# The opening of a float32 convolution and mixer kernel, worked in half chunks of two tokens

## The chip, the cores and the metric

The kernel runs on one core of a Trainium2 chip. The metric is the device time of one execution in microseconds (us), lower is better. The time before is the median of three runs.

## What is computed

The inputs are `x` of 8 batches x 4096 tokens x 192 features, `weight_gen` of 8 x 4096 x 8 heads x 7 taps, and four weight matrices that arrive as 64-bit floats. First comes a convolution over the last seven tokens, whose taps are a softmax; then a mixer over tokens and one over channels:

```python
w = softmax(weight_gen)                       # over the 7 taps, per token and head
out[b, s, h, :] = sum_k w[b, s, h, k] * x_pad[b, s + k, h, :]
h = relu(out.T @ w_tok1) @ w_tok2             # over the 4096 tokens, 256 hidden
u = out + h.T
y = u + relu(u @ w_ch1) @ w_ch2               # over the 192 features, 1536 hidden
```

## The kernel before, in words

A chunk is 512 tokens: each of the 128 partitions holds CT = 4 neighbouring tokens of 192 features. There are NCH = 8 chunks in a batch and NG = 64 in all. A main loop over the 64 chunks does the channel mixer on TensorE, and beside it the convolution and token mixing of later batches, in an order that a planner (`pump`) fixes when the program is built. Ahead of the loop stands the **prologue**, which is written out by hand: the convolution of the eight chunks of batch 0, their token mixing `th` (first product), and the conversion of the weights from 64-bit words to 32-bit floats. Each engine (and SyncE's DMA queue, SP, and GpSimd's, POOL) runs its instructions in the order in which this code issues them. Only the prologue and what first follows on it is touched.

For each chunk `m` the prologue of before goes like this.

- `softmax(m)` (L194) makes the taps of two chunks at once: on VectorE a maximum (L201) and a subtraction (L202), on ScalarE the exponential (L203), on VectorE the sum (L204), an addition, a reciprocal and a product (L210). `run(items, softmax(m + 1))` issues it from one place.
- `products(m)` (L344) multiplies the chunk with its taps on VectorE (L350): four taps in one instruction of 3072 elements a partition, three in one of 2304.
- `convert` (L157) turns raw words into floats: three ScalarE instructions (L170, L173, L174) and one on VectorE (L169, the `shift`). `begin` issues the ScalarE part of a weight block two chunks ahead, `run` the rest. Where a float is kept as two parts, `split` follows: a copy on ScalarE, a subtraction on VectorE (L188, L189). `convert_channel` does so for `w1` (three blocks) and `c2` (L495 to L497), `convert_w2` for the second token matrix.
- `sums(m)` (L362) adds the seven taps on TensorE, by 42 transposes that accumulate in PSUM (`tapsum`, L358); ScalarE copies the result to `sum` (L370); `turn_back` (L394) transposes it back, by six transposes, and ScalarE copies that to `xa` (L400).
- `token1_first` (L553) multiplies `xa` with the chunk's token weights on TensorE.
- `keep_sum` (L375) copies the transposed sum a second time from PSUM, by five ScalarE copies that sort the tokens (L388); for chunks 0 and 1 into the tiles `xb_`, from chunk 2 on into `ts`, which ScalarE's own DMA queue stores in DRAM (L391, L392). `load_xt` (L328) brings it back in the main loop.
- SP issues the loads of `x` (`load_x`), of the taps (`load_wg`), of raw weights (`fetch_...`; three raw buffers in turn), and the store `s0` of each converted token block (L959), in the order of the code; it waits where an instruction waits.

After the eight chunks `make_h1` (L507) applies the relu and splits `th` in two parts (L510 on ScalarE, L512 on VectorE), `token2(0)` (L558) makes the second token product (L570), VectorE adds it to chunk 0 (L580 to L582), and the main loop begins. PSUM of the main loop is the prologue's, so L570 waits for the last reader of `tapsum`.

Of the kernel before, what the change touches and what calls it, by code (L numbers as in the profile page):

```python
# [22 lines left out]
def mixer_kernel(ctx: ExitStack, tc: tile.TileContext, x, wg, wt1, wt2, wc1, wc2, out):  # L23
    nc = tc.nc
# [55 lines left out]
    def load_x(m):  # L80
# [12 lines left out]
        nc.gpsimd.memset(t[0:2, 0:PAD, :], 0.0)  # L93
# [22 lines left out]
    staged = {"raw": 0, "val": 0}  # L116
# [28 lines left out]
    def val_tile():  # L145

        n = staged["val"]
        staged["val"] += 1
        pool = pro if pro is not None and n % 6 >= 4 else p1
        return pool.tile([P, NV], F32, tag="val", name="val", bufs=2 if pool is pro else 4)  # L150
# [6 lines left out]
    def convert(raw, n, out):  # L157
# [5 lines left out]
        v = val_tile()[:, 0:n]  # L163
# [176 lines left out]


    KA = 4

    def products(m, pro):  # L344
        src, (wn, j) = xt.pop(m), wnt.pop(m)
        prs = []
        for k0, k1 in ((0, KA), (KA, K)):
            pr = pro.tile([P, KA, CT, D], F32, tag="pr", name="prk", bufs=3)[:, 0:k1 - k0]
            x_k, w = taps(src, wn, j, k0, k1)
            nc.vector.tensor_mul(pr.rearrange("p k t (h g) -> p k (t h) g", h=H), x_k, w)  # L350
            prs += [pr[:, k] for k in range(k1 - k0)]
        return prs

    sumt = {}
# [5 lines left out]
    NB = CT * D // P  # L360

    def sums(m, prs, between=lambda: None):  # L362

        ps = ps_pro.tile([P, 2, 512], F32, tag="sum", name="tapsum", bufs=2).rearrange("p k n -> p (k n)")
        for k, pr in enumerate(prs):
            flat = pr.rearrange("p t d -> p (t d)")
            for j in range(NB):
                transpose(ps[:, j * P:(j + 1) * P], flat[:, j * P:(j + 1) * P], k == 0 and j % 4 == 0)
        sumt[m] = p1.tile([P, CT, D], F32, tag="pr", name="sum", bufs=PR).rearrange("p t d -> p (t d)")
        nc.scalar.copy(sumt[m], ps[:, 0:NB * P])  # L370
        between()
        turn_back(m)
        return ps

    def keep_sum(m, ps):  # L375

        if m < 2:
            t = xbt[m] = xb_[m]
        else:
            t = pro.tile([P, 2, N], F32, tag="ts", name="ts0", bufs=2)  # L380
        to = [t[:, n, :].rearrange("p (n b t c) -> p c t n b" if m == 0 else "p (n t c b) -> p c t n b", c=2, t=2, b=Q)
              for n in range(2)]
        blocks = ps[:, 0:NB * P].rearrange("p (t j n b) -> p j t n b", t=2, n=P // Q, b=Q)
        lo, hi = slice(0, DC), slice(DC, P)
        for c in range(2):
            for n, rows, j, of in ((0, slice(0, P), 0, slice(0, P)), (1, hi, 1, lo)) if c == 0 else \
                    ((0, lo, 1, hi), (0, hi, 2, lo), (1, hi, 2, hi)):
                nc.scalar.copy(to[n][rows, c], blocks[of, j])  # L388
        if m >= 2:
            xst[m] = dram.tile([2, P, N], F32, name=f"xs{m}")  # L390
            nc.scalar.dma_start(xst[m][0], t[:, 0, :])  # L391
            nc.scalar.dma_start(xst[m][1, DC:P], t[DC:P, 1, :])  # L392

    def turn_back(m):  # L394

        t = sumt.pop(m)
        ps = ps_pro.tile([P, 2, 512], F32, tag="turn", name="turn").rearrange("p k n -> p (k n)")
        for j in range(NB):
            transpose(ps[:, j * P:(j + 1) * P], t[:, j * P:(j + 1) * P], j % 4 == 0)
        nc.scalar.copy(new_xa(m).rearrange("p c d -> p (c d)"), ps[:, 0:NB * P])  # L400

# [156 lines left out]
    def token2(m, up=None):  # L558
# [3 lines left out]
        if seeded:  # L562
            up = ps_w.tile([P, 2, 512], F32, tag="w", name="up")
            nc.scalar.copy(up.rearrange("p k (n b c) -> p (k n) c b", c=CT, b=Q),  # L564
                           xb.rearrange("p k (n c b) -> p (k n) c b", c=CT, b=Q))
# [346 lines left out]
    with tc.tile_pool(name="pro", bufs=1) as pro, \  # L912
# [5 lines left out]
        prefetch(0)  # L918
        th = ps_pro.tile([P, 2, 512], F32, tag="th", name="th")

        def token1_first(m, v):
            token1_float(th, v.rearrange("p (c r) -> p c r", c=CT), m,
                         0 if m == 0 else None, CT - 1 if m == NCH - 1 else None)

        def start(items):

            for item in items:
                if item[0] == "v":
                    return chain((item,), items)
                item[2]()  # L930

        begun = {}

        def begin(job, *what):
            v = []
            begun[what] = start(job(*what) if job else convert(rawt.pop(what), CT * R, v)), v

        extra = {2: ("w1", 0), 4: ("w1", 1)}
        run(softmax(0))
        fetch_w1(0)  # L940
        begin(None, "tok", 0)
        prefetch(1)
        fetch_w1(1)
        begin(None, "tok", 1)
        for m in range(NCH):
            prs = products(m, pro)
            if m + AHEAD < NCH:
                prefetch(m + AHEAD)
            items, (v,) = begun.pop(("tok", m))
            run(items, softmax(m + 1) if (m + 1) % SM == 0 and m + 1 < NCH else ())  # L950
            if m + AHEAD < NCH:
                fetch_w1(m + AHEAD)
            if m in extra:
                fetch_channel(*extra[m])
            if m == NCH - 2:
                load_wg(NCH)
                fetch_w2(0)
                fetch_channel("w1", 2)
            nc.sync.dma_start(s0[m], v)  # L959
            if m - 1 in extra:  # L960
                run(begun.pop(extra[m - 1])[0])
            if m < NCH - 1:
                ps = sums(m, prs)
                token1_first(m, v)
                keep_sum(m, ps)
            if m in extra:
                begin(convert_channel, *extra[m])
            if m + AHEAD < NCH:
                begin(None, "tok", m + AHEAD)
            if m == NCH - 2:  # L970
                begin(convert_w2, 0)
                begin(convert_channel, "w1", 2)
        fetch_channel("c2", 0)
        w2_items = begun.pop((0,))[0]
# [213 lines left out]
```

## Time and profile before

| what | us |
|---|---|
| median of three runs | 2113.66 (2111.83 to 2114.88) |
| span of the profiled execution, first to last instruction | 2109.4 |
| the median less that span | 4.3 |
| start of L580, which ends the prologue here | 126.06 |

The page gives no time of its own for the profiled execution beside its span; what lies around the span is taken as the 4.3 us of the table. All starts are counted from the first instruction. Busy is time in an instruction; instructions of one engine overlap by some hundredths of a us.

### The profile page before, as it was taken

The page shows a single profiled execution, that of the slowest core. Times are in us where ns is not written, and L with a number is a line of the kernel's source. Part 1 is how long each engine was busy: PE and PEld are TensorE (multiplying, and loading weights), DVE is VectorE, ACT ScalarE, POOL GpSimd, SP SyncE. Part 2 cuts the span into 40 slices and gives each one's busy share as a digit, 9 for nine tenths or more (in the row PEclk, how much of TensorE's full clock was granted, in tenths as well). Part 3 has the DMA queues.
Part 4 walks back from the last instruction along what each step waited for, and adds up shares of the span by engine and source line. Part 5 has one row for each costly group of instructions (what it writes and reads, how often), then busy time and mean ns, then how long its engine had stood idle before and what let it go on. Part 6 is the DMA issues. An engine that isn't in the chain of part 4 may idle for free.

```text
span 2109.4 us, 32249 instructions
## 1 busy us (share of the span) xinstructions
PE 2049.7 (97%) x12832; PEld 1686.3 (80%) x12832; DVE 1500.4 (71%) x1723; ACT 1449.9 (69%) x2245; POOL 159.5 (8%) x193
## 2 busy tenths in 40 slices
PE   6679999999999999999999999999999999999998
PEld 5667888788887888888888888888888888888887
DVE  6658988888888777777777787777777765343433
ACT  6578766677776676667667667666766766676665
POOL 0001111001101000000000010000100000000000
PEclk9899999999999999999999999999999999999999
DMA  8666767777876776666666666666666564321221
GB/s 321 198 204 189 210 169 227 229 206 204 243 225 165 204 200 172 188 158 181 175 197 174 191 181 167 174 184 200 177 184 191 147 170 140 91 71 49 57 63 23
DMA packets 165078, 363.82 MB, mean 172 GB/s; under 512 B 16456, under 2 KB 104264, under 8 KB 149568
## 3 DMA queue, kind: packets, MB, share of 16 engines
q1 hardware_dynamic: 138240, 284.96, 42.2%
q0 software_dynamic: 25344, 74.46, 18.2%
q10 hardware_dynamic: 1344, 2.36, 0.3%
q8 instruction: 100, 1.64, 0.3%
q14 instruction: 50, 0.41, 0.1%
HBM read 225.13 MB, written 70.52 MB: 140 GB/s over the span
## 4 chain that ended last, share of the span: by engine, by line
PE 79%; DVE 2%; DMA 1%; ACT 0%; issue 0%; ACTq 0%; SPq 0%; DVEq 0%
PE acc L653 35%; PE ph L635 32%; PE up L570 6%; PE th L533 4%; PE th L535 2%; DVE pr L233 1%; DVE h L642 0%; PE acc L670 0%; DMA out_dram<-out_tile 0%; DVE pr L247 0%; DMA xt<-in_x_dram 0%; DVE oc L710 0%; ACT up L564 0%; DVE oa L707 0%; DVE w L189 0%
## 5 line engine op out<-in xcount | busy, mean ns | idle before, releaser
L653 PE MATMUL acc<-h,w2s 128*128 128x512 f32 x3800 | 886.1, 390 | 2.0 <-DVE w2s L496 2.0
L653 PEld LDWEIGHTS acc<-h,w2s 128*128 128x128 f32 x3800 | 710.2, 188 | 148.8 <-DVE w2s L496 2.4
L641 ACT ACTIVATE h<-ph 128x1024 fp32r<-128x1024 f32 x384 | 394.4, 1027 | 349.5 <-PE ph L635 304.3
L642 DVE SCALAR_TENSOR_TENSOR h<-ph,h 128x1024 fp32r<-128x1024 f32 x384 | 468.4, 1220 | 120.1 <-ACT h L641 119.4
L635 PE MATMUL ph<-u_hi,w_hi 64*128 64x512 f32 x2304 | 338.7, 394 | 3.9 <-DVE h L642 2.6
L635 PE MATMUL ph<-u_lo,w_hi 64*128 64x512 f32 x2304 | 331.0, 388 | 0.6 <-ACT u_lo L610 0.3
L635 PE MATMUL ph<-u_hi,w_lo 64*128 64x512 f32 x2304 | 328.9, 387 | 0.0
L233 DVE TENSOR_TENSOR pr<-xt,wg 128x768 f32<-128x768 f32 x336 | 311.6, 947 | 0.2
L635 PEld LDWEIGHTS ph<-u_hi,w_hi 64*128 64x128 f32 x2304 | 214.4, 184 | 70.0 <-issue 19.4
L635 PEld LDWEIGHTS ph<-u_lo,w_hi 64*128 64x128 f32 x2304 | 219.9, 184 | 48.9 <-ACT u_lo L611 1.2
L635 PEld LDWEIGHTS ph<-u_hi,w_lo 64*128 64x128 f32 x2304 | 219.2, 184 | 46.9
L251 POOL DMA_DIRECT2D xa<-pr x168 | 146.1, 870 | 1410.1 <-DVE pr L247 798.2
L717 ACT COPY out_tile<-oa 32x256 f32<-32x256 f32 x504 | 203.5, 404 | 8.0
L582 DVE TENSOR_TENSOR uf<-up,uf 64x512 f32<-64x512 f32 x63 | 43.0, 683 | 213.0 <-ACT uf L578 213.0
L247 DVE TENSOR_TENSOR pr<-pr 128x768 f32<-128x768 f32 x168 | 160.2, 953 | 3.5
L570 PE MATMUL up<-w,h 128*128 128x512 f32 x630 | 161.0, 401 | 0.9 <-ACT up L564 0.8
L570 PEld LDWEIGHTS up<-w,h 128*128 128x128 f32 x630 | 114.2, 188 | 42.1 <-issue 13.8
L564 ACT COPY up<-xb 128x1024 f32<-128x1024 f32 x63 | 64.1, 1017 | 74.0 <-DVE h L642 67.4
L533 PE MATMUL th<-xh,w 128*128 128x384 f32 x384 | 112.5, 358 | 0.0
L292 DVE TENSOR_TENSOR xh<-xa,xh 128x768 fp32r<-128x768 f32 x48 | 45.8, 954 | 90.9 <-ACT xh L289 90.8
L717 ACT COPY out_tile<-oc 32x256 f32<-32x256 f32 x252 | 101.6, 403 | 8.0 <-DVE oc L710 3.5
L535 PE MATMUL th<-xh,w 128*128 128x192 f32 x384 | 96.2, 250 | 0.0
(87 smaller groups left out, 1647.1 us busy)
## 6 DMA issues: line engine op xcount, KB each, us to landing
w<-s SPq DMA_DIRECT2D x96, 1024.0 KB, 5.8
xa<-pr POOLq DMA_DIRECT2D x168, 384.0 KB, 5.2
xt<-in_x_dram SPq DMA_DIRECT2D x56, 960.0 KB, 9.8
out_dram<-out_tile SPq DMA_DIRECT2D x128, 192.0 KB, 5.9
xs<-t SPq DMA_DIRECT2D x56, 384.0 KB, 4.7
xb<-xs SPq DMA_DIRECT2D x336, 64.0 KB, 5.4
raw<-in_moe_w_tok_dram SPq DMA_DIRECT2D x16, 1024.0 KB, 9.3
s<-w POOLq DMA_DIRECT2D x8, 1024.0 KB, 4.8
```

Of the source, the lines that this page charges most:

```text
L233: nc.vector.tensor_mul(t.rearrange("p t (h g) -> p (t h) g", h=H).rearrange("p (o n) g -> p o n g", o=1), x_k, w)
L247: nc.vector.tensor_add(sums[m], sums[m], prt.pop(m))
L251: nc.gpsimd.dma_start(xat[m].rearrange("p t d -> p (t d)"), sums[m].rearrange("p t d -> p (t d)"), accum_op=ALU.add)
L533: nc.tensor.matmul(th[:, r, 0:2 * D], w[:, c, 0, rs], xh[:, c, :], start=i + c == 0, stop=False, skip_group_check=True)
L535: nc.tensor.matmul(th[:, r, 0:D], w[:, c, 1, rs], xh[:, c, 0:D], start=False, stop=c == CT - 1, skip_group_check=True)
L564: nc.scalar.copy(up.rearrange("p k (n b c) -> p (k n) c b", c=CT, b=Q), xb.rearrange("p k (n c b) -> p (k n) c b", c=CT, b=Q))
L570: nc.tensor.matmul(up[:, n, :], h1[:, k, d], w[:, l, k * N:(k + 1) * N], start=k == 0 and j == 0 and not seeded, stop=k == KR - 1 and j == ...
L635: nc.tensor.matmul(ph[:, j, :], w[rows, k, p * P:(p + 1) * P], u[rows, k], start=n == 0, stop=n == len(steps) - 1)
L641: nc.scalar.activation(h[:, :, 0, :], ph, AF.Relu)
L642: nc.vector.scalar_tensor_tensor(h[:, :, 1, :], ph, 0.0, h[:, :, 0, :].bitcast(F32), op0=ALU.max, op1=ALU.subtract)
L653: nc.tensor.matmul(acc[:, n, :], w2s[:, f, d], h[:, j, l, :], start=False, stop=f == NF - 1 and i == len(steps) - 1, skip_group_check=True)
L717: nc.scalar.copy(dst, src[to:to + Q].rearrange("p (n e d) -> p n e d", n=2, d=Q)[:, n])
```

## The change

The prologue is written anew, in 16 half chunks `i` of two tokens a partition.

- One VectorE product has all seven taps of a half chunk (2688 elements), three buffers in turn. 21 transposes sum it, 3 turn it back; `sum`, `xa` and the token product are made by halves, with two PSUM buffers of one bank for each.
- `token1_half(i - 1)` stands between `sums(i)` and `turn_back(i)` on TensorE.
- The sorted copies are gone. `store_sum` stores the untouched sum in DRAM, from GpSimd's queue; `load_xt` sorts blocks while loading, by five DMAs in place of two, also for chunks 0 and 1, and `token2` sorts tokens within a row as it reads.
- The next pair's softmax has its first three steps issued at `i % 4 == 0` and its others two halves later.
- The ScalarE steps of the conversions stand at the places that `steps` lists, between `keep_turned(i - 1)` and `keep_sum(i)`; their VectorE steps at those of `after`, behind the product. `loads` fixes the order of SP. The token blocks have five buffers `val` in the prologue's pool.
- The zeros ahead of the first chunk are written by VectorE in place of GpSimd.
- At the end the splits of `w2` and of `w1` block 1 stand before `make_h1`, `w1` block 2 and `c2` behind it.

```diff
-        nc.gpsimd.memset(t[0:2, 0:PAD, :], 0.0)
+        (nc.vector if m == 0 else nc.gpsimd).memset(t[0:2, 0:PAD, :], 0.0)
...
-            nc.sync.dma_start(t[:, 0, :], s[0])
-            nc.sync.dma_start(t[DC:P, 1, :], s[1, DC:P])
+            s = s.rearrange("p (h j n) -> p h j n", h=2, n=P)
+            to = t.rearrange("p k (h j n) -> p k h j n", h=2, n=P)
+            lo, hi = slice(0, DC), slice(DC, P)
+            for rows, k, j, of, block in ((slice(0, P), 0, 0, slice(0, P), 0), (lo, 0, 1, hi, 1), (hi, 0, 1, lo, 2),
+                                          (hi, 1, 0, lo, 1), (hi, 1, 1, hi, 2)):
+                nc.sync.dma_start(to[rows, k, :, j], s[of, :, block])
...
+    def product(i):
+        m, h = divmod(i, 2)
+        pr = prt[i] = pro.tile([P, K, HT, D], F32, tag="pr", name="prk", bufs=3)
...
+        nc.vector.tensor_mul(pr.rearrange("p k t (h g) -> p k (t h) g", h=H), x_k, w.broadcast_to([P, K, HT * H, G]))
...
+    def store_sum(m):
+        xst[m] = dram.tile([P, CT * D], F32, name=f"xs{m}")
+        nc.gpsimd.dma_start(xst[m], sumt.pop(m))
...
-            nc.vector.tensor_add(u[:, 0, :], up[:, 0, :], xb[:, 0, :])
-            nc.vector.tensor_add(u[c, 1, :], up[e, 1, :], xb[e, 1, :])
+            by_c = lambda a: a.rearrange("p (i c) -> p c i", c=CT)
+            for to, of, data in ((u[:, 0, :], up[:, 0, :], xb[:, 0, :]), (u[c, 1, :], up[e, 1, :], xb[e, 1, :])):
+                nc.vector.tensor_add(by_c(to), by_c(of), data.rearrange("p (c i) -> p c i", c=CT))
...
+        loads = {0: [tok[3]], 1: [3], 2: [tok[4]], 3: [4, "wg"], 4: ["s0", w1[0]], 5: [5], 6: ["s1", tok[5]], 7: [6],
+                 8: ["s2", tok[6]], 9: [7, tok[7]], 10: [w2], 11: [w1[1], "s3"], 12: [w1[2], "s4"], 13: [c2],
+                 14: ["xb", "wg1", "s5"], 15: [("c2", 1), ("w2", 1), "s6", "s7"]}
+        steps = {0: [(tok[0], 3)], 1: [(tok[1], 2)], 2: [(tok[1], 1), (tok[2], 1)], 3: [(tok[2], 2)],
+                 4: [(tok[3], 2)], 5: [(tok[3], 1), (tok[4], 1)], 6: [(tok[4], 2)], 7: [(w1[0], 3)], 8: [(tok[5], 3)],
+                 9: [(tok[6], 2)], 10: [(tok[6], 1), (w1[0], 1)], 11: [(tok[7], 3)], 12: [(w2, 3)],
+                 13: [(w1[1], 3)], 14: [(w1[2], 3)], 15: []}
+        after = {1: [tok[0]], 3: [tok[1]], 5: [tok[2]], 7: [tok[3]], 9: [tok[4], w1[0]], 11: [tok[5], w1[0]],
+                 12: [tok[6]], 13: [tok[7]]}
...
+        for i in range(2 * NCH):
+            product(i)
...
+            if i % 4 == 0 and i // 4 + 1 < len(soft):
+                run(islice(soft[i // 4 + 1], 3))
+            if i % 4 == 2 and i // 4 + 1 < len(soft):
+                run(soft[i // 4 + 1])
+            for what in after.get(i, ()):
+                dve(what)
+            sums(i)
+            if i > 0:
+                keep_turned(i - 1)
+            for what, n in steps[i]:
+                act(what, n)
+            keep_sum(i)
+            if i > 0:
+                token1_half(i - 1)
+            turn_back(i)
+            if i % 2 == 1:
+                store_sum(i // 2)
+            for what in loads[i]:
+                load(what)
+        keep_turned(i)
+        dve(w2)
+        rest(w2)
+        token1_half(i)
+        rest(w1[1])
         load_pair(NCH)
         make_h1(0, th[:, :, 0:D])
+        rest(w1[2])
+        rest(c2)
```

## Rows read from the trace of the kernel before

**Rows 1.** Busy time by engine in stretches: us, PE, PEld, DVE, ACT, POOL, granted clock, DMA share, GB/s.

```profile
0.00:10.00 10.00, 0.00 (x0) 0.00 (x0) 4.12 (x7) 2.06 (x3) 2.61 (x9) 1.00 0.72 214
...
20.00:30.00 10.00, 7.65 (x60) 7.39 (x61) 5.17 (x5) 8.93 (x12) 0.00 (x0) 1.00 1.03 422
...
80.00:90.00 10.00, 2.70 (x11) 2.28 (x11) 7.27 (x8) 5.28 (x10) 0.00 (x0) 0.62 0.72 184
...
sum 127.70, PE 81.38 PEld 75.13 DVE 81.20 ACT 79.10 POOL 4.88; mean PE 6.26 PEld 5.78 DVE 6.25 ACT 6.08 POOL 0.38
...
1200.00:1600.00 400.00, 400.00 (x2512) 328.66 (x2510) 295.53 (x347) 277.98 (x435) 32.79 (x38) 1.00 0.65 181
```

**Rows 2.** Who waited for whom, 0 to 135 us: total us, times, longest.

```profile
PE turn L358 <- ACT sum L370: 20.2, 8, 6.5
DVE mx L204 <- ACT wg L203: 19.8, 4, 8.9
```

**Rows 3.** Timeline of TensorE: start, us, instructions, count, idle time before.

```profile
12.53 7.19 PE L358 MATMUL tapsum<-ident,prk 128*128 128x128 f32 x42 [12.53 <-DVE prk L350]
...
25.93 4.75 PE L358 MATMUL tapsum<-ident,prk 128*128 128x128 f32 x42
31.57 0.87 PE L358 MATMUL turn<-ident,sum 128*128 128x128 f32 x6 [0.89 <-ACT sum L370]
33.33 2.87 PE L553 MATMUL th<-xa,val 128*128 128x192 f32 x16 [0.89 <-ACT xa L400]
...
59.81 5.49 PE L553 MATMUL th<-xa,val 128*128 128x192 f32 x16 [0.89 <-ACT xa L400]
...
121.33 4.64 PE L570 MATMUL acc<-w,h 128*128 128x512 f32 x10 [6.52 <-ACT ts L388]
```

**Rows 4.** Groups by line and form, 0 to 130 us: busy us, mean ns of one, idle before.

```profile
L350 DVE TENSOR_TENSOR prk<-xt,wg 128x3072 f32<-128x3072 f32 x8 | 26.8, 3353 | 1.8 <-DMA xt<-in_x_dram 1.8
...
L350 DVE TENSOR_TENSOR prk<-xt,wg 128x2304 f32<-128x2304 f32 x8 | 20.4, 2552 | 0.4 <-PE tapsum L358 0.4
...
L388 ACT COPY ts<-tapsum 64x256 f32<-64x256 f32 x24 | 8.8, 366 | 0.4
...
L388 ACT COPY xb<-tapsum 64x256 f32<-64x256 f32 x8 | 4.0, 494 | 0.1
```

**Rows 5.** Timeline of ScalarE, its first conversion and its last.

```profile
12.35 1.16 ACT L170 ACTIVATE few<-raw 128x1024 uint32<-128x1024 uint32 x1 [7.12 <-DMA raw<-in_moe_w_tok_dram]
...
110.03 1.05 ACT L188 CAST w<-val 128x1024 fp32r<-128x1024 f32 x1
...
113.98 0.92 ACT L170 ACTIVATE few<-raw 128x768 uint32<-128x768 uint32 x1
...
116.62 0.48 ACT L510 ACTIVATE h<-th 128x384 fp32r<-128x384 f32 x1
```

**Rows 6.** Timeline of VectorE, start and end of the prologue.

```profile
9.11 5.83 DVE L350 TENSOR_TENSOR prk<-xt,wg 128x3072 f32<-128x3072 f32 x2 [1.76 <-DMA xt<-in_x_dram]
15.92 1.23 DVE L169 SCALAR_TENSOR_TENSOR val<-val,few 128x1024 uint32<-128x1024 uint32 x1 [0.98 <-ACT val L174]
...
117.13 0.62 DVE L512 SCALAR_TENSOR_TENSOR h<-th,h 128x256 fp32r<-128x256 f32 x2 [2.07 <-ACT h L510]
117.67 0.95 DVE L169 SCALAR_TENSOR_TENSOR val<-val,few 128x768 uint32<-128x768 uint32 x1
...
119.86 0.69 DVE L497 TENSOR_TENSOR w2s<-val,w2s 128x512 fp32r<-128x512 f32 x1
...
126.06 0.69 DVE L580 TENSOR_TENSOR uf<-acc,xb 128x512 f32<-128x512 f32 x1 [4.33 <-PE acc L570]
```

**Rows 7.** Timeline of SP's queue, the second load of chunk 0.

```profile
3.25 0.30 SPq L95 DMA_DIRECT2D xt<-in_x_dram  x1
```

**Rows 8.** DMA issues over the whole span: count, KB each, median us from issue to landing.

```profile
xa<-pr POOLq DMA_DIRECT2D x168, 384.0 KB, 5.2
...
raw<-in_moe_w_tok_dram SPq DMA_DIRECT2D x16, 1024.0 KB, 9.3
```

More of the change, by code (lines that the diff above doesn't have):

```diff
@@ L143, in few_tile, with val_tile, convert @@
         return few["both"][:, few["next"], 0:n].bitcast(U32)
[L145 to L157, printed above, removed]
+    def val_tile(own=False):
+        pool = pro if own else p1
+        return pool.tile([P, NV], F32, tag="val", name="val", bufs=5 if own else 4)
+    def convert(raw, n, out, own=False):
         yield "gate", 0, lambda: state["vals"] < 2 and state["few"] == 0
@@ L339, in load_xt @@
                               s[:, d, :].rearrange("(n a) j -> a n j", a=Q))
[L342 to L352, printed above, removed]
@@ L356, in transpose @@
+    sumt, sum_ps, turn_ps = {}, {}, {}
     def transpose(out, data, start):
         nc.tensor.matmul(out, data, ident, is_transpose=True, start=start, stop=True, skip_group_check=True)
[L360 to L366, printed above, removed]
-            for j in range(NB):
[L368 to L392, printed above, removed]
@@ L394, in turn_back, with sums @@
-    def turn_back(m):
-        t = sumt.pop(m)
-        ps = ps_pro.tile([P, 2, 512], F32, tag="turn", name="turn").rearrange("p k n -> p (k n)")
-        for j in range(NB):
-            transpose(ps[:, j * P:(j + 1) * P], t[:, j * P:(j + 1) * P], j % 4 == 0)
-        nc.scalar.copy(new_xa(m).rearrange("p c d -> p (c d)"), ps[:, 0:NB * P])
+    def sums(i):
+        pr = prt.pop(i)
+        ps = sum_ps[i] = ps_pro.tile([P, 512], F32, tag="sum", name="tapsum", bufs=2)
+        flat = pr.rearrange("p k t d -> p k (t d)")
+        for k in range(K):
+            for j in range(NB):
+                transpose(ps[:, j * P:(j + 1) * P], flat[:, k, j * P:(j + 1) * P], k + j == 0)
@@ new lines, in keep_sum, with turn_back @@
+    def keep_sum(i):
+        m, h = divmod(i, 2)
+        if h == 0:
+            sumt[m] = p1.tile([P, CT, D], F32, tag="pr", name="sum", bufs=PR).rearrange("p t d -> p (t d)")
+        nc.scalar.copy(sumt[m][:, h * HC:(h + 1) * HC], sum_ps.pop(i)[:, 0:HC])
+    def turn_back(i):
+        m, h = divmod(i, 2)
+        data = sumt[m][:, h * HC:(h + 1) * HC]
+        ps = turn_ps[i] = ps_pro.tile([P, 512], F32, tag="turn", name="turn", bufs=2)
+        for j in range(NB):
+            transpose(ps[:, j * P:(j + 1) * P], data[:, j * P:(j + 1) * P], j == 0)
@@ L917, in mixer_kernel @@
         nc.scalar.activation(warm, ident[:, 0:1], AF.Exp)
-        prefetch(0)
+        load_wg(0)
+        load_x(0)
         th = ps_pro.tile([P, 2, 512], F32, tag="th", name="th")
[L921 to L929, printed above, removed]
-                item[2]()
@@ L932, in mixer_kernel @@
[L932 to L955, printed above, removed]
-                load_wg(NCH)
[L957 to L972, printed above, removed]
@@ L973, in mixer_kernel, with job @@
-        fetch_channel("c2", 0)
-        w2_items = begun.pop((0,))[0]
-        run(islice(w2_items, 2))
-        fetch_channel("c2", 1)
-        ps = sums(m, prs, lambda: run(w2_items))
-        token1_first(m, v)
-        run(begun.pop(("w1", 2))[0])
-        fetch_w2(1)
+        jobs, vals = {}, {}
+        def job(what):
+            if what not in jobs:
+                if what[0] == "tok":
+                    vals[what[1]] = []
+                    jobs[what] = iter(convert(rawt.pop(what), CT * R, vals[what[1]], True))
+                else:
+                    jobs[what] = iter(convert_w2(what[1]) if what[0] == "w2" else convert_channel(*what))
+            return jobs[what]
@@ new lines, in act, with dve, rest, token1_half @@
+        def act(what, n=1):
+            for item in job(what):
+                item[2]()
+                n -= item[0] in "asu"
+                if n == 0:
+                    return
+        def dve(what, n=1):
+            for item in job(what):
+                item[2]()
+                n -= item[0] == "v"
+                if n == 0:
+                    return
+        def rest(what):
+            for item in job(what):
+                item[2]()
+        def token1_half(i):
+            m, h = divmod(i, 2)
+            w = vals[m][0].rearrange("p (c r) -> p c r", c=CT)
+            for r in range(KR):
+                for c in range(HT * h, HT * h + HT):
+                    nc.tensor.matmul(th[:, r, 0:D], w[:, c, r * P:(r + 1) * P], xat[m][:, c, :],
+                                     start=m + c == 0, stop=m == NCH - 1 and c == CT - 1, skip_group_check=True)
@@ new lines, in store_val, with fetch @@
+        def store_val(m):
+            nc.sync.dma_start(s0[m], vals[m][0])
+        def fetch(what):
+            fetch_w1(what[1]) if what[0] == "tok" else fetch_w2(what[1]) if what[0] == "w2" else fetch_channel(*what)
+        tok = [("tok", m) for m in range(NCH)]
+        w1 = [("w1", n) for n in range(3)]
+        w2, c2 = ("w2", 0), ("c2", 0)
+        soft = [softmax(m) for m in range(0, NCH, SM)]
+        fetch(tok[0])
+        load_wg(SM)
+        load_x(1)
+        fetch(tok[1])
+        load_x(2)
```

45 lines of the change are left out of this document (37 added, 8 removed).

## Prediction

> **What bounds the kernel now.** I read the busy time by stretches first. From 1200 to 1600 us TensorE is busy 400.00 of 400 us: the main loop is TensorE's own work, and nothing of its products changes. The opening is another matter: over the first 127.7 us TensorE, VectorE and ScalarE are busy 81.38, 81.20 and 79.10 us, so none of the three is full [rows 1]. What the opening costs is that they wait for each other in turn, and it is worth as much as L580 (the addition that hands over to the main loop) starts earlier; it starts at 126.06 now, as the table has it.
>
> The waits say where the turns are [rows 2]. TensorE waits 20.2 us in eight chunks for the copy of the sum before it can turn it back. VectorE waits 19.8 us in four softmaxes for the exponential, because ScalarE has all conversions of the next blocks ahead of it. Behind the longer of these stops TensorE's clock falls: from 80 to 90 us it is busy 2.70 of 10 us at a granted 0.62 [rows 1], and the 16 products of one chunk take 5.49 us where they take 2.87 at full clock [rows 3]. These are the two levels, 1.2 and 2.4 GHz.
>
> **The change, part by part.** TensorE's work is only divided. At full clock 42 transposes take 4.75 us, 16 token products 2.87 and 6 transposes back 0.87 [rows 3], so a half chunk takes 2.38 + 1.44 + 0.44 = 4.26 us and the 16 halves 68.1 us. A product of 2688 elements lies midway between the two present forms, 3353 and 2552 ns [rows 4]: 2.95 us, and 16 of them 47.2, the sum of the two groups now (26.8 + 20.4). The work of VectorE stays.
>
> The sorted copies go: 8.8 + 4.0 us in their two larger groups [rows 4], and ScalarE's DMA issues. They were not what the chunks waited for, but they stood between evictions. In return evictions come in halves of 384 elements, 0.48 us each by L510, which has that size [rows 5].
>
> What now sets the pace of a half is the loop TensorE, ScalarE, TensorE. While TensorE sums half `i` (2.38) and does the token product of `i - 1` (1.44), ScalarE copies `xa` (0.48), does its conversion steps and copies the sum (0.48). Three steps of 1024 elements took 3.57 us, from 12.35 [rows 5] to 15.92 [rows 6], which makes 0.48 + 3.57 + 0.48 + 0.44 for the turn = 4.97 us, 0.7 more than TensorE's 4.26; this is so in halves 8, 11 and 12. Three steps of 768 took 2.64 us (113.98 to 116.62 [rows 5]) and fit under 4.26, as do two steps. VectorE has two products, a shift of 1.23 and a quarter of the four softmaxes a chunk, less than TensorE's 8.5; with three buffers it runs ahead. The exponential is issued two halves before its result is asked for, so the 19.8 us go; late next on that path is the product itself, for which TensorE would wait.
>
> **The start.** SP sits at L95 until 3.25 us [rows 7], because GpSimd clears the strip ahead of chunk 0 late. VectorE is idle then; I take 1 us earlier for every load behind it (bounds 0 and 2, the row's 3.25 less the loads before it). So the first product starts at 8.1 in place of 9.11 and ends at 11.1. The first turn back needs the first sum's copy, which stands behind the exponential and three conversions of a block that lands at about 11.4 (12.35 less 1). The exponential waits for the second pair's taps, now loaded behind that block, so ScalarE begins at about 13.5 and the turn at 13.5 + 3.57 + 0.48, about 18 us (bounds 15.5 and 20). From there TensorE has 68.1 - 2.4 = 65.7 us left: 83.7. The clock is low at first; the first 42 transposes took 7.19 against 4.75 now [rows 3], so 2.4 more. The three halves of 4.97 add 2.1, the last eviction 0.6: token mixing ends at about 89 and the last copy of `xa` at 87.5.
>
> **The end.** Now a chain of ScalarE and VectorE follows: `w2` copied 1.05 [rows 5] and subtracted (as a shift, 1.23), `w1` block 1 shifted 0.95, copied (1.05 x 768/1024 = 0.79) and subtracted 0.95, `make_h1` 2 x 0.62 [rows 6]: 6.2 us, to 93.7. Behind it in VectorE's queue, ahead of L580, stand the rest of `w1` block 2 (0.95 + 0.79), the three steps of `c2` (2.64) and its rest, which took 2.88 from 117.67 to the end of L497 [rows 6]: 7.3 us, to 101. L570 took 4.64 even at the low clock [rows 3] and ends at 98.3, under it. So L580 starts at 101 if no load is late.
>
> **The loads.** A raw buffer comes free when the block three before it is converted. Token block 6 can be asked for after block 4's steps in half 6 and is used in half 9: some 2.5 halves or 10.7 us, where landing takes 9.3 at the median [rows 8]; block 5 and `w1` block 2 (six issues) stand alike. A slack of one or two us does not always hold; I take 1 us for each of the three: L580 at 104. The rate itself suffices: the blocks needed by then (ten of 1024 KB, eight `x` of 960, four of 768, some 2 MB of `s0` and taps, and six stored sums) are about 27 MB, and 10 us at 214 and the rest at 422 GB/s [rows 1] bring them by 69 us.
>
> **What costs nothing.** The stores of sums from GpSimd: such an issue lands in 5.2 us under a busy VectorE in the main loop [rows 8], and its first reader, the load for chunks 0 and 1, comes some ten halves later; without that cover 5.2 us. The ten DMAs of that load stand on SP ahead of the loads for block 1 of `c2` and `w2`, needed only in the main loop; see the third rival. Strided additions into `u`: no row has them on VectorE; ScalarE's strided copies took 494 against 366 ns for 256 elements [rows 4], so between 0 and 0.5 us for both; I take none, since L580 to the first product has other work beside it.
>
> **Sum.** 126.06 - 104 = 22 us off a span of 2109.4, 2087.4; with the 4.3 us between span and median, 2091.7. All later instructions are the same, on a TensorE that is full, so I expect the 22 us to be kept.
>
> **The rivals.** *Loads late.* If landing takes 12 us in place of 9.3, as it may when loads, stores of `s0` and sums come in 90 us in place of 126, each of the blocks 5 to 7, `w2` and two of `w1` delays its half by some 1.5 to 2.5 us more: L580 at 116, 2103. For it: the DMA share is 1.03 from 20 to 30 us [rows 1]. Against: it is so only because loads run ahead there.
>
> *The clock, slower.* The half chunks put TensorE's work into shorter groups with an eviction between them. If it runs at 1.2 GHz for half of the 68.1 us, 34 us are added: L580 at 138, 2126. It decides from 22 / 68.1 on, a third of the work at the low level. Against it: from 20 to 30 us TensorE is busy 7.65 of 10 us with waits of 0.89 before each turn and each token product [rows 3], and the granted clock is 1.00 [rows 1]; after the change its waits are shorter. For it: any stop as long as those now, and the first two halves, which begin low. The Trainium skill ("TensorE: Matmul & The Clock Gate", section "A second HAM failure mode: psum-queue depth-cycling") speaks against this change: it says that frequent short idling between groups of matmuls, as PSUM buffers are cycled, makes the clock swing between its levels. By that rule this rival's 2126 would be the forecast; the row at 1.00 speaks against it.
>
> *Given back.* The main loop needs block 1 of `c2` and `w2` soon after it begins, and these loads come behind ten small DMAs and with two stores of `s0`. If they or the attention of batch 1 are due at the same time as before, TensorE waits there: no change, 2113. Against: their raw buffers come free with halves 13 and 14, as far ahead of L580 as now.
>
> **How the numbers follow.** Forecast 0.62, its own range 2086 (no late load, a start 1 us better) to 2098; late loads 0.20; given back 0.09; the clock 0.09. About 0.2%, 4 us, is what a measurement of this kernel can tell from no change. Faster by more: 0.62 + 0.20 = 0.82; within: 0.09; slower: 0.09. The range takes in the forecast and the late loads: 2085 to 2105.
>
> **What would show it.** L580 at 100 to 108 us; `turn` waiting for `sum` well under 20.2 us; no long wait of L204; TensorE at a granted 0.95 or more from 30 us to the end of token mixing, with the 21 transposes at 2.4 us; L570 not behind an eviction. It is wrong if ScalarE's first conversion steps wait for raw blocks in most halves, if TensorE's transposes double in time, or if L580 comes earlier and a later wait of `acc` or `ph` takes it back.

## The result and the profile after

The changed kernel takes 2085.39 us at the median (2085.02 to 2086.05, four runs), against 2114.27 (2111.83 to 2116.59) for the kernel before beside it: a ratio of 0.9866, with an interval of 0.9852 to 0.9880.

| what | before | after |
|---|---|---|
| span of the profiled execution, us | 2109.4 | 2083.5 |
| start of the hand-over addition into `u` (L580, now L583) | 126.06 | 99.55 |
| start of the first main-loop product `ph` (L635, now L637) | 127.67 | 101.35 |
| from there to the end of the span | 1981.7 | 1982.2 |

The hand-over comes 26.5 us earlier, `ph` 26.3, and the span is 25.9 shorter: what the opening gained, the main loop kept. The medians differ by 28.9. The profile of before is one of its quicker executions; in the executions timed beside the last runs below its spans go from 2108.5 at a granted clock of 0.992 to 2112.8 at 0.989, so the time of before goes with its clock; in which stretch the clock fell there was recorded for the profiled execution alone.

Busy time of the changed kernel in stretches, with the columns of [rows 1]:

```profile
20.00:30.00 10.00, 9.68 (x77) 9.24 (x76) 9.90 (x9) 7.36 (x10) 1.28 (x2) 1.00 1.02 417
...
50.00:60.00 10.00, 6.65 (x53) 6.06 (x52) 9.90 (x9) 6.96 (x10) 0.54 (x1) 1.00 0.99 403
...
80.00:90.00 10.00, 6.72 (x48) 5.87 (x46) 2.46 (x3) 4.24 (x8) 2.12 (x3) 1.00 0.86 268
...
sum 97.70, PE 72.94 PEld 67.86 DVE 78.22 ACT 63.49 POOL 7.74; mean PE 7.29 PEld 6.79 DVE 7.82 ACT 6.35 POOL 0.77
```

VectorE does nearly the same work, 78.22 us against 81.20, but in 97.7 us in place of 127.7; from 16.86 to 77.48 us it is busy 60.24 of 60.62 us, so for these sixty it is the engine that is full. ScalarE has 15.6 us less. The clock stays at 1.00 from 20 to 90 us. The waits of its opening:

```profile
DVE w L187 <- ACT w L186: 9.2, 1, 9.2
POOL uf L1045 <- DMA xt<-in_x_dram: 8.3, 1, 8.3
PE turn L362 <- ACT sum L378: 7.6, 6, 1.8
...
DVE mx L202 <- ACT wg L201: 0.6, 1, 0.6
```

The exponential's 19.8 us of [rows 2] are 0.6, and that from the first softmax alone. The wait at the turn fell from 20.2 to 7.6, its longest from 6.5 to 1.8, and behind none of these stops did the clock fall. The timeline of TensorE, which answers to [rows 3]:

```profile
10.98 4.71 PE L362 MATMUL tapsum<-ident,prk 128*128 128x128 f32 x21 [10.98 <-DVE prk L356]
17.25 0.55 PE L362 MATMUL turn<-ident,sum 128*128 128x128 f32 x3 [1.56 <-ACT sum L378]
...
35.22 2.46 PE L362 MATMUL tapsum<-ident,prk 128*128 128x128 f32 x21
37.52 1.47 PE L957 MATMUL th<-xa,val 128*128 128x192 f32 x8
38.82 0.49 PE L362 MATMUL turn<-ident,sum 128*128 128x128 f32 x3
39.15 2.46 PE L362 MATMUL tapsum<-ident,prk 128*128 128x128 f32 x21
...
52.83 0.55 PE L362 MATMUL turn<-ident,sum 128*128 128x128 f32 x3 [1.81 <-ACT sum L378]
...
85.72 1.57 PE L957 MATMUL th<-xa,val 128*128 128x192 f32 x8 [0.57 <-ACT xa L393]
91.28 3.86 PE L571 MATMUL acc<-w,h 128*128 128x512 f32 x10 [3.99 <-DVE h L510]
...
101.35 3.36 PE L637 MATMUL ph<-u_hi,w_hi 64*128 64x512 f32 x6 [4.83 <-ACT u_hi L607]
```

A half in which ScalarE has two conversion steps takes 39.15 - 35.22 = 3.93 us, and TensorE has no wait in it. Where three steps of 1024 elements stand before the copy of the sum, the turn waits, as at 52.83; with three of 768 it does not. The token products end at 87.29. The end on VectorE, with the last copy of `xa` on ScalarE, the strip `uf` on GpSimd and the late issues of SP:

```profile
90.52 0.61 DVE L510 SCALAR_TENSOR_TENSOR h<-th,h 128x256 fp32r<-128x256 f32 x2
...
97.76 0.68 DVE L495 TENSOR_TENSOR w2s<-val,w2s 128x512 fp32r<-128x512 f32 x1
98.36 0.61 DVE L199 TENSOR_REDUCE mx<-wg 128x64 f32<-128x448 f32 x1
...
99.55 2.15 DVE L583 TENSOR_TENSOR uf<-acc,xb 128x512 f32<-128x512 f32 x2
...
85.19 0.48 ACT L393 COPY xa<-turn 128x384 f32<-128x384 f32 x1 [1.15 <-PE turn L362]
...
98.07 0.52 POOL L1045 MEMSET uf<- 64x512 f32 x1 [8.33 <-DMA xt<-in_x_dram]
...
72.43 7.78 SPq L336 DMA_DIRECT2D xb<-xs  x10
...
84.28 1.27 SPq L961 DMA_DIRECT2D s<-val  x2
```

VectorE has no idle time before L583: it stands behind what is queued there, 8 us after `make_h1`. Just below that lies something that the prediction had not seen: GpSimd may clear `uf` only at 98.07. The experiments come back to it.

### The profile page after: what moved, and what is told of

Same layout as the page of the kernel before. It is cut to its first block, busy times and chain, and to the rows that moved or that the text cites. A ratio compares the mean times of both kernels' runs of the same rounds, so it can differ in the third digit from the quotient of the medians.

```text
span 2083.5 us, 32275 instructions
## 1 busy us (share of the span) xinstructions
PE 2041.8 (98%) x12832; PEld 1679.5 (81%) x12832; DVE 1501.5 (72%) x1724; ACT 1435.4 (69%) x2221; POOL 163.3 (8%) x200
## 4 chain that ended last, share of the span: by engine, by line
PE 78%; DVE 3%; DMA 1%; ACT 0%; issue 0%; ACTq 0%; SPq 0%; DVEq 0%
PE acc L655 35%; PE ph L637 31%; PE up L571 7%; PE th L531 4%; PE th L533 2%; DVE h L644 1%; DVE pr L231 1%; PE acc L672 0%; DMA out_dram<-out_tile 0%; DVE pr L245 0%; DMA xt<-in_x_dram 0%; ACT up L565 0%; DVE oc L712 0%; DVE xa L231 0%; DVE oa L709 0%
## 5 line engine op out<-in xcount | busy, mean ns | idle before, releaser
L637 PE MATMUL ph<-u_hi,w_hi 64*128 64x512 f32 x2304 | 339.5, 395 | 7.9 <-ACT u_hi L607 4.8
L637 PE MATMUL ph<-u_lo,w_hi 64*128 64x512 f32 x2304 | 331.1, 388 | 0.6 <-ACT u_lo L612 0.3
L637 PE MATMUL ph<-u_hi,w_lo 64*128 64x512 f32 x2304 | 329.2, 387 | 0.0
L637 PEld LDWEIGHTS ph<-u_hi,w_hi 64*128 64x128 f32 x2304 | 215.1, 185 | 74.5 <-issue 19.4
L637 PEld LDWEIGHTS ph<-u_lo,w_hi 64*128 64x128 f32 x2304 | 219.9, 184 | 48.5 <-ACT u_lo L613 0.9
L637 PEld LDWEIGHTS ph<-u_hi,w_lo 64*128 64x128 f32 x2304 | 219.3, 184 | 46.9
L571 PE MATMUL up<-w,h 128*128 128x512 f32 x630 | 160.9, 401 | 1.6 <-ACT up L565 1.2
L571 PEld LDWEIGHTS up<-w,h 128*128 128x128 f32 x630 | 114.2, 188 | 42.8 <-issue 13.4
L565 ACT COPY up<-xb 128x1024 f32<-128x1024 f32 x56 | 57.0, 1017 | 67.2 <-DVE h L644 65.8
## 6 DMA issues: line engine op xcount, KB each, us to landing
raw<-in_moe_w_tok_dram SPq DMA_DIRECT2D x16, 1024.0 KB, 12.7
```

Source lines behind the costliest of these rows:

```text
L571: nc.tensor.matmul(up[:, n, :], h1[:, k, d], w[:, l, k * N:(k + 1) * N], start=k == 0 and j == 0 and not seeded, stop=k == KR - 1 and j == ...
L637: nc.tensor.matmul(ph[:, j, :], w[rows, k, p * P:(p + 1) * P], u[rows, k], start=n == 0, stop=n == len(steps) - 1)
```

## The experiments

Three runs make parts of the change alone in the kernel before (e1 to e3), the others alter the changed kernel. The marker is the start of `ph`; "addition" is the hand-over addition.

| run | addition | `ph` | span | median us | ratio to before (interval) |
|---|---|---|---|---|---|
| before, softmax early (e1) | 120.64 | 122.28 | 2103.8 | 2104.47 | 0.9959 (0.9944 to 0.9974) |
| before, unsorted sums (e2) | 116.17 | 117.99 | 2097.6 | 2100.47 | 0.9942 (0.9928 to 0.9957) |
| before, both (e3) | 106.30 | 108.13 | 2089.3 | 2090.71 | 0.9892 (0.9875 to 0.9908) |
| after | 99.55 | 101.35 | 2083.5 | 2085.39 | 0.9866 (0.9852 to 0.9880) |
| after, softmax at once (e4) | 102.65 | 104.46 | 2087.5 | 2088.39 | 0.9883 (0.9868 to 0.9897) |
| after, not interleaved (e5) | 103.18 | 105.00 | 2087.7 | 2089.45 | 0.9887 (0.9871 to 0.9904) |
| after, copies added (e6) | 102.96 | 104.75 | 2088.6 | 2089.44 | 0.9889 (0.9875 to 0.9904) |
| after, GpSimd's zeros (e7) | 102.19 | 104.00 | 2084.6 | 2087.16 | 0.9881 (0.9865 to 0.9896) |
| after, end retimed (e8) | 100.67 | 102.48 | 2083.7 | 2085.02 | 0.9869 (0.9854 to 0.9884) |
| e8, stores ahead (e9) | 93.11 | 94.94 | 2077.5 | 2077.08 | 0.9830 (0.9815 to 0.9845) |
| after, stores ahead (e10) | 98.71 | 100.50 | 2083.1 | 2085.99 | 0.9872 (0.9854 to 0.9890) |

### e1: the softmax early, in the kernel before

```diff
-            run(items, softmax(m + 1) if (m + 1) % SM == 0 and m + 1 < NCH else ())
+            run(items)
+            if m % SM == 0 and m + SM < NCH:
+                soft_of[m + SM] = softmax(m + SM)
+                run(islice(soft_of[m + SM], 3))
+            if m + 1 in soft_of:
+                run(soft_of.pop(m + 1))
```

> The kernel before, with one part of the change alone: the first three steps of the next pair's softmax are issued at the even chunk, the others at the odd one. Marker: start of the first main-loop product ph, 127.67 us before and 101.35 after the change. Theory A (the opening is a chain of turns, and VectorE's stop behind the exponential is its largest link): VectorE's wait for the exponential falls from 19.8 us to under 4, and ph starts 12 to 16 us earlier, near 114. Rival B (the gain is ScalarE's work that goes, the sorted copies and DMA issues): the wait moves to another place, ph starts under 5 us earlier, 123 or later.

`ph` came 5.4 us earlier, between the two expectations. Its waits, from 0 to 122 us:

```profile
PE turn L358 <- ACT sum L370: 14.8, 8, 3.5
DVE val L169 <- ACT val L174: 14.2, 4, 5.7
```

The wait for the exponential is down to 0.6 us, and VectorE now waits 14.2 us in all, against 7.4 before, for ScalarE's conversions instead: it came sooner to the next thing that ScalarE owed it. Theory A had the link, but took a wait in a chain for a gain of its own size.

### e2: unsorted sums, in the kernel before

The sorted copies go, `load_xt` and `token2` read as in the change, and the sum is stored at once:

```diff
     def keep_sum(m, ps):
-        for c in range(2):
...
-                nc.scalar.copy(to[n][rows, c], blocks[of, j])
...
+        xst[m] = dram.tile([P, CT * D], F32, name=f"xs{m}")
+        nc.gpsimd.dma_start(xst[m], kept_sum.pop(m))
```

> The kernel before, with the other separable part alone: no sorted copies on ScalarE, the untouched sum stored from GpSimd's queue, blocks sorted while loading. Theory A: only what stood in a turn comes back, some 1.9 us at the exponential of three chunks and at L570's wait, in all 6 to 8 us: ph starts near 120. Rival B (ScalarE's work): the whole 15 us of copies and the DMA issues with them, ph at 110 or earlier.

9.7 us: some more than theory A's 6 to 8, far from B's 17. VectorE waits 15.1 us for the exponential where it waited 19.8, and L563 no longer stands behind the sorted copies (3.1 us behind `make_h1` in place of 6.52 [rows 3]):

```profile
ACT sum L374 <- PE tapsum L362: 23.6, 5, 7.1
...
DVE mx L204 <- ACT wg L203: 15.1, 4, 6.3
...
PE acc L563 <- DVE h L502: 3.1, 1, 3.1
```

ScalarE has the time now and waits for TensorE with it, 23.6 us.

### e3: both in the kernel before

The edits of e1 and e2 together.

> Both parts of the two runs before together, chunks still whole and conversions where they were. Theory A: near the sum of the two, 18 to 20 us, ph near 108, so 6 to 8 us are left for the half chunks and the places of the conversions. Rival C (the half chunks and the interleaved token product carry the gain): under 10 us, ph at 118 or later.

19.5 us, within theory A's 18 to 20, and 4.4 more than 5.4 + 9.7: with one wait gone the other still held the chain. The clock has a part in this that was not measured apart: in stretches of 10 us it still falls to 0.66 in e1 (20 to 30 us) and in e2 (80 to 90), while in e3 it reads 1.00 from 30 to 97.7 us. `ph` is 6.8 us from the changed kernel's, and that is what the rest of the change is worth together: half chunks, the interleaved token product, the places of the conversions and loads, the order of the end, and VectorE's zeros. Rival C is refuted: three quarters of the 26.3 us come with whole chunks.

### e4: the softmax at one place, in the changed kernel

```diff
-            if i % 4 == 0 and i // 4 + 1 < len(soft):
-                run(islice(soft[i // 4 + 1], 3))
             if i % 4 == 2 and i // 4 + 1 < len(soft):
```

> The changed kernel with all steps of a softmax issued at one place, two halves later. Theory A: VectorE waits again for the exponential behind ScalarE's conversions, 3 to 5 us in each of three softmaxes; its lead of up to three products covers part, so ph starts 5 to 10 us later than 101.35. Rival C: TensorE's loop alone sets the pace and covers it: 0 to 2 us.

3.1 us, below the expected 5 to 10 and above the rival's 2. VectorE waits for the exponential 5.9 us in four softmaxes, 3.4 at most, in place of 19.8: by the order of the code the exponential stands behind the conversion steps of one half now, at most three.

```profile
DVE mx L202 <- ACT wg L201: 5.9, 4, 3.4
...
56.76 1.12 ACT L168 ACTIVATE few<-raw 128x1024 uint32<-128x1024 uint32 x1 [3.29 <-DMA raw<-in_moe_w_tok_dram]
...
59.63 0.55 PE L362 MATMUL turn<-ident,sum 128*128 128x128 f32 x3 [3.08 <-ACT sum L378]
60.02 4.12 PE L362 MATMUL tapsum<-ident,prk 128*128 128x128 f32 x21
```

These waits alone cost TensorE nothing up to half 9: it starts at 52.79 here and at 53.22 in the changed kernel. The loss comes then, by a longer path. VectorE has by then waited 1.22 and 0.65 us for exponentials, and product 7 ends 0.95 us later here. The load of `x` that waits for it goes out at 43.76 in place of 42.81, and behind it on SP that of raw block 6 at 44.79 in place of 43.71. Its conversion waits 3.29 us in place of 1.70, the turn 3.08 in place of 1.54, and after that stop the 21 transposes take 4.12 us in place of 2.46 (granted clock 0.83 from 60 to 70 us). At half 11 the run is 2.8 us behind. So theory A's direct cost did not show, and the rival missed what a small delay on VectorE does through SP's queue.

### e5: the token product not between sum and turn

```diff
             keep_sum(i)
-            if i > 0:
-                token1_half(i - 1)
             turn_back(i)
+            if i > 0:
+                token1_half(i - 1)
```

> The changed kernel with the token product of the half before put behind the turn back, not ahead of it, so that nothing covers the copy of the sum. Theory (TensorE and ScalarE in turn set the pace of a half): 0.5 to 0.6 us more in each of 16 halves, ph starts 8 to 10 us later than 101.35. Rival (VectorE sets the pace): under 2 us.

3.65 us, under half of what was expected. Two halves on TensorE:

```profile
37.19 2.46 PE L362 MATMUL tapsum<-ident,prk 128*128 128x128 f32 x21
40.21 0.55 PE L362 MATMUL turn<-ident,sum 128*128 128x128 f32 x3 [0.57 <-ACT sum L378]
40.60 1.47 PE L957 MATMUL th<-xa,val 128*128 128x192 f32 x8
41.90 2.46 PE L362 MATMUL tapsum<-ident,prk 128*128 128x128 f32 x21
```

A half with two conversion steps takes 41.90 - 37.19 = 4.71 us where the interleaved order takes 3.93: the uncovered copy of 0.57 is there in each, as the theory had it. But halves 11 and 12, where ScalarE has three steps of 1024 elements, take 4.96 in both orders; and the three halves that take 5.23 to 5.96 in the changed kernel, behind an exponential or a raw block, take 4.71 to 4.97 here: the slower pace hides the stop. Fourteen halves from the second on take 67.2 us here and 63.4 there. The changed kernel does not hold 3.93 for long either, because VectorE's products come 4.38 us apart on average, as the account of the prediction shows below; that this is why so little was lost fits the rows, but no run tried it apart.

### e6: ScalarE's copies added to the changed kernel

```diff
+        if h == 1:
+            t = pro.tile([P, 2, 256], F32, tag="ts", name="ts0")
+            for j, rows in enumerate((P, DC, DC, DC, DC)):
+                nc.scalar.copy(t[0:rows, j % 2], sumt[m][0:rows, 0:256])
```

The scratch tile that they write is read by nothing.

> The changed kernel with five ScalarE copies of 256 elements a chunk added behind the copy of the odd half's sum, as much ScalarE time as the sorted copies were (about 0.37 us each, 15 us in all). Theory: ScalarE is busy 63.5 of the first 97.7 us, so about half of it falls into its idle time: ph starts 5 to 8 us later. Rival (ScalarE's work is the bound): 13 to 15 us. Rival (it is off the path): under 2 us.

The copies took 13.9 us, and `ph` came 3.4 later, less than the 5 to 8 of the theory: three quarters fell into idle time. Part of the 3.4 is the clock: two groups of 21 transposes, at 18.41 and 54.87 us behind stops of 2.88 and 2.03 at the turn, take 3.60 and 4.12 us in place of 2.46. In the kernel before the same kind of work was worth 9.7 us (e2). That speaks for the copies' place as their price, ahead of the conversions and of the exponential in a queue that others waited for. It does not prove it: these copies read `sum`, where those of before read PSUM, for which L570 waited, and the DMA issues are not in this run.

```profile
L382 ACT COPY ts<-sum 64x256 f32<-64x256 f32 x32 | 10.6, 408 | 0.0
L382 ACT COPY ts<-sum 128x256 f32<-128x256 f32 x8 | 3.3, 410 | 0.0
```

### e7: GpSimd's zeros back

```diff
-        (nc.vector if m == 0 else nc.gpsimd).memset(t[0:2, 0:PAD, :], 0.0)
+        nc.gpsimd.memset(t[0:2, 0:PAD, :], 0.0)
```

> The changed kernel with the strip of zeros ahead of chunk 0 cleared by GpSimd again. Theory: all loads behind it go out 1.1 us later, and the first product starts 1 us later than 7.88; ph starts 1 us later than 101.35. Rival: the first pairs wait for other loads anyway, ph moves by less than 0.3 us.

SP issues L95 at 3.26 us in place of 2.15; the first product starts at 8.27 in place of 7.88, the second, behind the next pair's taps, at 14.15 in place of 12.74. Neither the theory's 1 us at the first product nor its 1 us at `ph` came true. The edit is worth about 1.4 us at the start of the chain, and `ph` is 2.65 later. The first turn waits 2.63 us in place of 1.56, and the 21 transposes after it take twice as long, 2.2 us more:

```profile
19.36 4.68 PE L362 MATMUL tapsum<-ident,prk 128*128 128x128 f32 x21
```

Stops in halves 3 and 4 of the changed kernel fall away in return, so the last token product starts only 1.9 us later; a wait of the addition on a DMA, 0.63, makes up most of the rest. By the medians alone this run is not told from the changed kernel (2085.61 to 2090.41).

### e8: the end in another order

```diff
-                 13: [(w1[1], 3)], 14: [(w1[2], 3)], 15: []}
+                 13: [(w1[1], 3)], 14: [(w1[2], 3)], 15: [(w2, 1), (w1[1], 1)]}
...
-                 12: [tok[6]], 13: [tok[7]]}
+                 12: [tok[6]], 13: [tok[7]], 14: [w2], 15: [w1[1]]}
...
-        dve(w2)
-        rest(w2)
-        token1_half(i)
-        rest(w1[1])
+        act(c2)
+        dve(w1[2])
+        rest(w2)
+        rest(w1[1])
+        token1_half(i)
...
-        rest(c2)
+        act(c2, 2)
         soft = softmaxes()
         run(islice(soft, 2, 4))
+        dve(c2)
+        act(c2)
...
     run(first, second)
+    rest(c2)
+    state["vals"] = 0
```

> The changed kernel with its end put in another order: the shifts of w2 and w1 block 1 behind the last two products, their copies in half 15, the shift of w1 block 2 ahead of the last token product, the conversion of c2 split round the hand-over, its subtractions behind the additions. Theory (the chain of ScalarE and VectorE behind the last half holds the hand-over, 13.9 us from the last copy of xa to L583): the hand-over addition starts at 92 to 94 in place of 99.55, ph at 94 to 96 in place of 101.35, and the time falls by 5 to 7 us to about 2079. Rival: the main loop's first needs (c2, w1 block 2, late loads) take it back: same time, with a later wait of acc or ph longer by as much.

Neither came true. VectorE was ready by 92.4, L571 done by 92, and then all waited; `ph` came at 102.48 and the time did not change, but the wait is not in the main loop. It is at the addition itself:

```profile
100.67 2.17 DVE L583 TENSOR_TENSOR uf<-acc,xb 128x512 f32<-128x512 f32 x2 [8.24 <-DMA xt<-in_x_dram]
...
100.76 0.52 POOL L1048 MEMSET uf<- 64x512 f32 x1 [13.46 <-DMA xt<-in_x_dram]
...
73.25 9.49 SPq L336 DMA_DIRECT2D xb<-xs  x10
...
86.86 1.73 SPq L961 DMA_DIRECT2D s<-val  x2
```

GpSimd's clearing of `uf` waits to the same time, so it looks like the tile's memory that is not free; e9 tries this. The tile belongs to a pool that the main loop opens where the prologue's pool was. The prologue's token blocks `val` lay there, and the last two are read until their stores `s6` and `s7` land. Those are issued at 86.86 to 88.6 us, behind ten small loads `xb` that hold SP for 9.49 us and behind two loads of weights, and land 13.1 us after issue, at about 100 to 101, by the view of DMA issues from 86.8 to 88.62 us:

```profile
s<-val SPq DMA_DIRECT2D x2, 512.0 KB, 13.1
```

This is when `uf` is cleared. The DMA that the rows name, a load of `x`, is another of the same queue; e9 speaks to it. In the changed kernel the same pair is issued at 84.28 and lands 13.0 later, at 98: 98.07 is where its `uf` is cleared.

### e9 and e10: the stores ahead, with and without the new end

Both alter SP's order alone; e9 on top of e8, e10 on the changed kernel. In both, the taps of the next batch, one block each of `c2` and `w2`, and the ten loads in two groups follow the stores.

```diff
-                 8: ["s2", tok[6]], 9: [7, tok[7]], 10: [w2], 11: [w1[1], "s3"], 12: [w1[2], "s4"], 13: [c2],
-                 14: ["xb", "wg1", "s5"], 15: [("c2", 1), ("w2", 1), "s6", "s7"]}
+                 8: ["s2", tok[6]], 9: [7, tok[7]], 10: [w2], 11: [w1[1], "s3"], 12: [w1[2], "s4", "s5"], 13: [c2, "s6", "s7"],
+                 14: ["wg1", ("c2", 1), "xb"], 15: [("w2", 1), "xb1"]}
...
             if what == "xb":
                 load_xt(0)
+            elif what == "xb1":
                 load_xt(1)
```

> The kernel with the end retimed (run e8), and on SP's queue the last three stores of token blocks ahead of the ten small loads for chunks 0 and 1, of which chunk 1's five go last. Theory (in e8 the main loop's tile uf lies where the prologue's token blocks lay, so it waits for the stores s6 and s7, issued at 86.9 to 88.6 us and landing 13.1 later): the stores land by 85, VectorE's hand-over addition starts at 92 to 93.5 and ph at 93.5 to 95.5, 7 us ahead of 101.35; the time falls by 5 to 7 us, to 2078 to 2080. Rival (another buffer, or the loads of x for batch 1, hold it): the addition stays at 100 or later, same time.

> The changed kernel with only SP's order altered as in e9, the end as it was. Theory (two waits end close together there, VectorE's chain at 99.55 and the stores at 98): VectorE's chain is still there, the hand-over addition starts at 98 to 99.6, and the time falls by less than 1.5 us. Rival (the stores alone hold the hand-over): the addition starts at 95 or earlier.

The additions start as the theory had it in both. In e9 the stores are issued by 76.8, the addition starts at 93.11 straight behind VectorE's own work, with no wait, and the time is 2077.08 us, 0.9830 of before; its runs go from 2074.06 to 2079.26, all below those of the changed kernel (2085.02 to 2086.05); the median is a little better than the 2078 to 2080 that were expected. The loads of `x` for the next batch did not hold `uf`: the first of them is issued at 92.20, after `uf` was cleared at 91.97.

```profile
74.60 2.22 SPq L961 DMA_DIRECT2D s<-val  x2
...
92.24 0.95 DVE L167 SCALAR_TENSOR_TENSOR val<-val,few 128x768 uint32<-128x768 uint32 x1
93.11 2.19 DVE L583 TENSOR_TENSOR uf<-acc,xb 128x512 f32<-128x512 f32 x2
...
91.97 0.52 POOL L1049 MEMSET uf<- 64x512 f32 x1 [3.94 <-ACT val L172]
```

In e10 `uf` is cleared earlier, at 94.79, and VectorE's queue still holds the addition to 98.71; its median, 2085.99, is not told from the changed kernel's. So two waits ended within two us of each other at the hand-over; by the start of `ph`, either removed alone gives nothing (e8) or 0.8 us (e10), both give 6.4.

```profile
97.52 0.61 DVE L199 TENSOR_REDUCE mx<-wg 128x64 f32<-128x448 f32 x1
...
98.71 2.16 DVE L583 TENSOR_TENSOR uf<-acc,xb 128x512 f32<-128x512 f32 x2
...
94.79 0.52 POOL L1046 MEMSET uf<- 64x512 f32 x1 [5.89 <-issue]
```

## Why the prediction was right, and where its terms were off

The forecast was 2091.7 us in a range of 2085 to 2105; the time is 2085.39, at the range's lower end, and L583 starts at 99.55, just ahead of the 100 to 108 that were to show it. The mechanism held: the opening was a chain of turns, the change took the turns apart, and TensorE's main loop kept the gain. One reading in it was wrong: VectorE does not run ahead, it is full, and it bounds the pace of a half. That the time still fell into the range is in part luck, as several terms were off in opposite directions. The sum by its steps:

- **A half chunk, 4.26 us.** It is 3.93. The term added durations, and instructions of one engine overlap: 2.46 + 1.47 + 0.49 make 4.42 in the rows of after, yet the next half starts after 3.93. Over 16 halves that is 5 us. Against it stood more halves held up than the three that were named: that of the third exponential (5.23 from 29.99 to 35.22) and the one after the raw block. From the second half on, 14 halves take 81.07 - 17.64 us, 4.53 each.
- **VectorE "runs ahead".** It does not. Two products, a shift and half a softmax are 5.90 + 1.23 + 1.61 = 8.7 us a chunk (the softmax's six steps are 3.22 us for two chunks), which is more than TensorE's 8.5, not less. In the trace its products 2 to 14 start (70.52 - 18.01) / 12 = 4.38 us apart, and VectorE has no idle time between. In halves 2 to 8 TensorE begins a sum 0.1 to 1.3 us after its product ends, and the exponentials of halves 4 and 8 are late because ScalarE waits for VectorE's subtraction:

```profile
18.01 2.95 DVE L356 TENSOR_TENSOR prk<-xt,wg 128x2688 f32<-128x2688 f32 x1
...
70.52 5.82 DVE L356 TENSOR_TENSOR prk<-xt,wg 128x2688 f32<-128x2688 f32 x2
...
31.07 0.58 ACT L201 ACTIVATE wg<-wg 128x448 f32<-128x448 f32 x1 [2.08 <-DVE wg L200]
...
48.01 0.58 ACT L201 ACTIVATE wg<-wg 128x448 f32<-128x448 f32 x1 [1.19 <-DVE wg L200]
```

  From half 9 on TensorE is 2.2 to 4.7 us behind the products; there halves with three steps of 1024 and the late block count. Up to the last sum a faster ScalarE could so have won back at most 4.7 us, an estimate from these rows.
- **The start.** The first product starts at 7.88 (8.1 forecast), the first turn at 17.25 (18). The slow start is there: the first 21 transposes take 4.71 us, later ones 2.46. The granted clock of that stretch reads 1.00, in before as well, so only these durations show it.
- **Late loads, 3 us.** One conversion waited for a raw block, 1.70 us:

```profile
55.60 1.16 ACT L168 ACTIVATE few<-raw 128x1024 uint32<-128x1024 uint32 x1 [1.70 <-DMA raw<-in_moe_w_tok_dram]
```

  It is block 6, one of the three named; the other two were in time.
- **The end.** The last copy of `xa` ends at 85.67 (87.5), token mixing at 87.29 (89), `make_h1` at about 91.1 (93.7), `c2` at 98.4 (101). The chain from `xa` on has nearly the forecast's length, 12.8 us against 13.5; the 0.62 that the forecast took twice for `make_h1` is one row of two instructions, and ScalarE's 0.48 stands beside it. Forgotten were two steps of the next softmax ahead of the addition, 1.2 us.
- **The strided additions**, put at 0 to 0.5 us: the two take 2.15 us, where L580 and L581 of before start at 126.06 and 126.78 and take 0.69 each, 1.41 in all. So 0.7 us are added, outside the bound, which came from ScalarE's copies.
- **The sorted copies**, "not what the chunks waited for": taken out alone they gave 9.7 us (e2), by the exponential and by L570, which waited 6.52 us for the last of them. No term of the sum rests on this.
- **Span to median, 4.3 us.** It is 1.7 in the changed kernel's profiled execution (2085.23 for a span of 2083.5). The term took the gap between a quick execution of before and the median of others for work around the span.

So 104 for L583 was 99.55: some 0.8 us from the start, 1.3 from the late loads, 2.6 from the halves (what is then left to the end of token mixing), 0.7 to 0.9 from the chain at the end, less 1.2 for the softmax forgotten. Of the 6.3 us by which the time was missed the work around the span is 2.6.

Of the rivals, late loads cost 1.70 us where 12 more were priced. The premise of that rival, a landing after 12 us, came true all the same. The profile gives a landing for two of the ten token loads in the opening, with this median:

```profile
raw<-in_moe_w_tok_dram SPq DMA_DIRECT2D x10, 1024.0 KB, 12.7
```

Block 6, asked for at 43.71, was there at 55.60, some 12 us later. What failed was the count: the other blocks were asked for early enough, and one of six came late. The clock did not fall: 1.00 from 20 to 90 us, with halves of four us and stops of at most 1.8. The margin was small: in e4 and e6 the transposes behind stops of 3.08 and 2.03 us at the turn took 4.12 us, at a granted clock of 0.83 over those 10 us. The rule that was weighed against the change (the Trainium skill, "TensorE: Matmul & The Clock Gate", section "A second HAM failure mode: psum-queue depth-cycling") does not describe this trace: the groups of matmuls are shorter than before and PSUM buffers change twice as often, but the stops between them are fewer and shorter, and the clock is the steadier. Nothing was given back behind the hand-over. The third rival had SP's ten small DMAs and the stores behind them in view, but for the main loop's loads; they held something else, the memory of the prologue's pool, and cost nothing only because VectorE's queue ended 1.5 us later.

## What to carry to other kernels

A wait in a chain of turns is not a gain of its own size: here the wait for the exponential and the sorted copies, each taken out alone, gave 5.4 and 9.7 us, together 19.5, and at the hand-over one of two gave nothing. So before an edit, look for the wait that ends next, and that includes the memory: where one pool was opened over another here, the first write of the new one waited for the last store of the old, and loads ahead of that store in its queue delayed it. Before calling an engine ahead, add up all that its queue holds for one unit of work. Price a stretch of one engine by the distance between starts in the timeline, not by the sum of durations.

## What was not expected of the hardware

Ten small loads hold SP's queue for 7.78 us in the changed kernel and 9.49 in e8, five for 5.28 to 6.01 in e9 and, after the hand-over, for 3.14 in the changed kernel: 0.63 to 1.20 us each, where one load of `x`, 960 KB, is issued in 0.33. What makes the small ones cost so much was not tried. Of the two stores of 512 KB issued from 84.28 us on, the one whose landing the profile gives landed 13.0 us after issue, no sooner than the 1024 KB loads of the same opening (12.7, against 9.3 in before [rows 8]).
